# New numbers for a list scheduler: later loads, reserved buffers, gates and priorities in a recurrence + MoE kernel

## The chip, the cores and the metric

The kernel runs on one core of a Trainium2 chip. The metric is the device time of one execution in microseconds (us). The kernel before was timed three times: 1112.65, 1116.74 and 1118.03 us, median 1116.74 us. The kernel after is to be timed in the same way.

## The reference

What is computed is a recurrence over 768 steps for 4 batches of 8 heads with 40 dimensions, followed by two feed-forward networks on the 3072 x 320 result:

```
for t in range(S):
    y[:, :, t] = einsum('bhd,bhde->bhe', r_t, state)
    Sa = einsum('bhde,bhe->bhd', state, a_t)
    state = state * w_t[:, :, None, :] - einsum('bhd,bhe->bhde', Sa, b_t) + einsum('bhd,bhe->bhde', v_t, k_t)
x = y as 3072 x 320
x = relu(x @ w_in) ** 2 @ w_out                 # 320 -> 2048 -> 320   (MLP1)
out = (((x @ w1) * (x @ w2)) @ w3) @ w_out2     # 320 -> 1024 -> 320   (MLP2)
```

The weights of the two networks come in as 64-bit floats.

## The kernel before

**Units and chunks.** The recurrence is cut into 12 chunks of 64 steps, and each chunk into 4 batches. One batch of one chunk is a unit; there are 48, and unit u belongs to chunk u // 4. Two neighbouring units share a pair r = u // 2 and with it the loads of `w` and `a`; `kb` (k and b together) is loaded for each unit. Within a chunk the recurrence is a triangular system: `kn` (L384) builds it from `xl` (a times a running product of w) and `kb`, the two 32x32 halves of it are inverted, and `xu` is solved by four groups of small matmuls (L586, L600, L621, L635). `kbt` (L654) turns `kb` over, L697 makes `m`, L749 and L754 the output `y`, L723 the new state, and L668 turns state and solution over. On VectorE stand the scans of w (L310), the scaling of `kb` (L359), `xl` (L368) and the masked halves of `kn` (L394).

**The inverse.** From chunk 1 on one chain of 62 VectorE operations (31 times L526 and L531, each on the result of the one before) inverts the blocks of all four units of a chunk at once. The result `pt` goes out to DRAM (`dt`) and back in another layout (`tt`); L600 and L635 of these units read it. Chunk 0 is inverted in another way, level by level.

**MLP1 and MLP2.** When the four units of a chunk have left their `y`, it goes through DRAM (`xd`, `xraw`), is turned over and split into a high and a low part (`xh`, `xlo`), and goes through MLP1: L1016 `h` (L975 for chunk 0, with `gt` at L984), `g`, `gh` and `gl`, and the accumulation over 2048 columns at L1053 to L1055 (`acc`). MLP1 of a chunk lies beside the recurrence of later chunks. MLP2 comes at the end: the product of w3 and its output matrix (`w3p`, L1269) first, then `ab` (L1411) and `o` (L1443 to L1445). The weights are decoded by ScalarE, VectorE and GpSimd (L1620 to L1632).

**What sets the order.** Each piece of work is a step with an engine, a cost, what it reads and writes, and the buffers that it takes. `emit` (class `Plan`) puts the steps into one order with a simulated clock: on a free engine the ready step goes first whose rank is the highest. The rank is the longest chain of costs behind the step plus a weight, and the weight is `PR[kind] - later * SLOPE`, with `later` growing with the unit or the chunk. A step that needs a buffer goes only when its pools have room: `k2` has 35 buffers, `bank` has the 8 PSUM banks. `SPARE[kind]` says how many of them have to stay free after such a step; a lighter step must leave more. Before, every kind has 33 of `k2` and 6 banks there, and a flag `tight` drops all these reserves for good at the first moment at which nothing else can go. The program then issues the instructions in that order, and each engine runs its own in order. SyncE issues nearly all loads, in one order too.

**Idle matmuls.** Where the simulated clock leaves TensorE empty for longer than `IDLE`, up to the last decisive step of chunk 0's MLP1, matmuls of the identity with itself (L1119, `idle`) fill the gap. Their results are not used.

**Gates.** A load of `kb` and `a` for unit u waits in the plan for `at{u - 8}`, which is the `xu` matmul (L586) of that earlier unit; a load of `w` for pair r waits for `at{2r - 10}`.

The lines are shifted by four in the kernel after: L1016 is L1012 there, L384 is L380, L1119 is L1115.

Of the kernel before, what the change touches and what calls it, by code (L numbers as in the profile page):

```python
# [23 lines left out]
class Plan:  # L24
# [28 lines left out]
    def emit(self):  # L53
        st = self.steps
        n = len(st)
# [10 lines left out]
        used, free, dma = Counter(), dict.fromkeys("SGVAP", 0.0), 0.0  # L66
        ready, wait = [0.0] * n, {e: [] for e in "SGVAP"}
        for i, k in enumerate(st):
            if not left[i]:
                for e in k[0]:  # L70
                    wait[e].append(i)
        events, ends, order, tight = [0.0], [], [], False
        port, other = dict(V=0.0, G=0.0), dict(V="G", G="V")
        self.log = []

        def fits(i):
            take, out, opens = Counter(), [], {x for x, _ in st[i][4]}
# [12 lines left out]
        while len(order) < n:  # L90
            if not events:

                assert not tight, ("no room", used)
                tight = True
                events.append(t)
            t = heappop(events)
            while ends and ends[0][0] <= t + 1e-9:
                x = heappop(ends)[1]
# [3 lines left out]
            for e in "SGVAP":  # L102
                while free[e] <= t + 1e-9:
# [14 lines left out]
                    i, k = best, st[best]  # L118
# [40 lines left out]
def rwkv_moe(tc, wE, wF, wL, aE, kbE, rE, vE, vX, mask_d, ident_d, id32_d, eye_d, lev_d, sel_d, w_in, w_out, w1, w2, w3T, wo2_d,  # L159
             rS, kS, vS, wS, aS, bS, out):  # L160
    nc = tc.nc
    V, A, G, T, S = nc.vector, nc.scalar, nc.gpsimd, nc.tensor, nc.sync
# [69 lines left out]
    def load_w(r):  # L232
        if not once("w", r, NPAIR):
            return

        def go(tag):
            pw[r] = room(tag, [128, 8, 8, 8], f"w{r}")
            S.dma_start(out=pw[r].rearrange("p q s i -> p (q s i)"), in_=wE[r])
        step("S", 0.73, go, (f"at{2 * r - 10}",), (f"w{r}",), new=((f"w{r}", ("k2",)),))

    def load_unit(u):
        if not once("kb", u, NU):
            return
        r = u // 2

        def go(tag):
            ukb[u] = room(tag, [128, NP, 2, C], f"kb{u}")
            S.dma_start(out=ukb[u].rearrange("p q k t -> p (q k t)"), in_=kbE[u])

        def go_a(tag):  # L250
            pa[r] = room(tag, [128, 2, NP, C], f"a{r}")
            S.dma_start(out=pa[r].rearrange("p e q t -> p (e q t)"), in_=aE[r])
        step("S", 0.73, go, (f"at{u - 8}",) if u >= 8 else (), (f"kb{u}",), new=((f"kb{u}", ("k2",)),))
        if u % 2 == 0:
            step("S", 0.73, go_a, (f"at{u - 8}",) if u >= 8 else (), (f"a{r}",), new=((f"a{r}", ("k2",)),))
# [535 lines left out]
    wi = [mp.tile([128, FF], F32R, tag=f"wi{k}", bufs=1, name=f"wi{k}") for k in range(5)]  # L791
    wo = []
# [291 lines left out]

    LEAD, ITEMS = 5, 6

    PR = {'z': -1968, 'first': -376, 'l1': -4516, 'p0': -439, 'p1': 500, 'p2': -1417, 'p3': -257, 'v0': -362, 'v1': -2000, 'v2': -1452, 'v3': -2387, 'c0': -333, 'c1': -1230, 'c2': -2317, 'c3': -4652, 'o0': -1654, 'o1': 640, 'o2': -2216, 'o3': -2665, 'wi': -212, 'wo': -350, 'h0': -435, 'h1': -246, 'moe': -1909, 'st': -2657, 'pr': -2642, 'cv': -2226, 'm2': -2729}
    SPARE = {'z': {'k2': 33, 'bank': 6}, 'first': {'k2': 33, 'bank': 6}, 'l1': {'k2': 33, 'bank': 6}, 'p0': {'k2': 33, 'bank': 6}, 'p1': {'k2': 33, 'bank': 6}, 'p2': {'k2': 33, 'bank': 6}, 'p3': {'k2': 33, 'bank': 6}, 'v0': {'k2': 33, 'bank': 6}, 'v1': {'k2': 33, 'bank': 6}, 'v2': {'k2': 33, 'bank': 6}, 'v3': {'k2': 33, 'bank': 6}, 'c0': {'k2': 33, 'bank': 6}, 'c1': {'k2': 33, 'bank': 6}, 'c2': {'k2': 33, 'bank': 6}, 'c3': {'k2': 33, 'bank': 6}, 'o0': {'k2': 33, 'bank': 6}, 'o1': {'k2': 33, 'bank': 6}, 'o2': {'k2': 33, 'bank': 6}, 'o3': {'k2': 33, 'bank': 6}, 'wi': {'k2': 33, 'bank': 6}, 'wo': {'k2': 33, 'bank': 6}, 'h0': {'k2': 33, 'bank': 6}, 'h1': {'k2': 33, 'bank': 6}, 'moe': {'k2': 33, 'bank': 6}, 'st': {'k2': 33, 'bank': 6}, 'pr': {'k2': 33, 'bank': 6}, 'cv': {'k2': 33, 'bank': 6}, 'm2': {'k2': 33, 'bank': 6}}
    SLOPE = 0.832
    pl = Plan({**{k: v[1] for k, v in POOLS.items()}, "ur0": 1, "ur1": 1}, PR["st"], dict(V=V, G=G, A=A))  # L1090
    plan.append(pl)

    def go(kind, later, fn, *args):
        pl.kind = kind, later
        pl.weight = PR[kind] - later * SLOPE
        pl.spare = SPARE.get(kind, {})
        return fn(*args)
# [213 lines left out]
    n = 0  # L1311
# [410 lines left out]
```

## Time and profile before

| | before |
|---|---|
| median of 3 runs | 1116.74 us |
| profiled execution | 1114.61 us |
| its span | 1112.4 us |
| mean granted TensorE clock | 0.972 |
| PE busy | 1048.4 us (94%) |
| DVE busy | 730.2 us (66%) |
| ACT busy | 550.8 us (50%) |
| POOL busy | 118.9 us (11%) |
| chain that ended last | PE 79%, DVE 7%, DMA 5% |

The profiled execution took 2.2 us more than its span, and 2.1 us less than the median. In the profile PE is TensorE's matmuls, PEld its weight loads, DVE VectorE, ACT ScalarE, POOL GpSimd, SP or SPq SyncE and its DMA queue. A matmul's row shows when it began and how long it took; since matmuls overlap, the pitch (from one begin to the next) says what it costs. The profile keeps two records for each fp32 matmul, so a count of x34 is 17 matmuls.

### The profile page before, as it was taken

The numbers are of one execution on the slowest core, as the hardware profiler recorded it, in microseconds if no ns is written. First come the engines' busy times: TensorE is split into PE (matmuls) and PEld (weight loads), VectorE is DVE, ScalarE is ACT, GpSimd is POOL, SyncE is SP. The second block draws the span as 40 slices with busy tenths as digits, with TensorE's granted clock in tenths as the row PEclk, the third lists the DMA queues.
The fourth block names the chain that finished last, engine by engine and source line by source line (L and its number), as shares of the span: only waits on it lengthen the run. The fifth ranks groups of instructions, "written<-read, shape, count | busy, mean of one in ns | idle before, by whom it ended". The sixth has DMA issues, their size and how long they took to land.

```text
span 1112.4 us, 28437 instructions
## 1 busy us (share of the span) xinstructions
PE 1048.4 (94%) x11416; PEld 963.2 (87%) x11416; DVE 730.2 (66%) x1929; ACT 550.8 (50%) x1233; POOL 118.9 (11%) x178
## 2 busy tenths in 40 slices
PE   8999925999999899999999999999999999999996
PEld 8899825888989789898978999999998888888885
DVE  7878988877787778787888856257777332323321
ACT  3545522555555555656465665566665222222221
POOL 4442100000000000000000000023333000000000
PEclk9999966999999999999999999999999999999998
DMA  9754132534243444434525242344444310100000
GB/s 287 210 164 143 34 98 69 155 79 125 83 121 88 115 110 113 121 98 121 141 67 151 79 99 62 95 132 147 142 144 124 93 29 24 32 21 24 1 24 27
DMA packets 150403, 111.05 MB, mean 100 GB/s; under 512 B 61688, under 2 KB 130296, under 8 KB 150264
## 3 DMA queue, kind: packets, MB, share of 16 engines
q1 hardware_dynamic: 150264, 109.16, 35.4%
q8 instruction: 92, 1.51, 0.6%
q14 instruction: 47, 0.39, 0.1%
HBM read 91.88 MB, written 17.24 MB: 98 GB/s over the span
## 4 chain that ended last, share of the span: by engine, by line
PE 79%; DVE 7%; DMA 5%; ACT 2%; issue 2%; SPq 1%; POOL 1%; POOLq 0%; ACTq 0%; DVEq 0%
PE ab L1411 16%; PE h L1016 14%; PE acc L1053 4%; PE m L697 4%; PE acc L1055 4%; PE acc L1054 4%; PE kn L384 3%; PE o L1445 2%; PE o L1444 2%; PE o L1443 2%; PE w3p L1269 2%; PE idle L1119 2%; PE y L754 2%; PE y L749 2%; PE xu L586 2%
## 5 line engine op out<-in xcount | busy, mean ns | idle before, releaser
L1411 PE MATMUL ab<-x,w 128*128 128x512 f32 x768 | 183.3, 391 | 0.0
L1411 PEld LDWEIGHTS ab<-x,w 128*128 128x128 f32 x768 | 142.1, 188 | 27.4
L1016 PE MATMUL h<-xh,wi 128*128 128x256 f32 x880 | 140.9, 291 | 3.4 <-ACT xh L942 2.5
L1016 PEld LDWEIGHTS h<-xh,wi 128*128 128x128 f32 x880 | 120.0, 193 | 5.9 <-ACT xh L942 2.7
L1053 PE MATMUL acc<-wo,gh 128*128 128x320 f32 x384 | 125.0, 325 | 0.0
L1431 DVE TENSOR_TENSOR as<-ab,as 128x512 f32<-128x512 f32 x48 | 33.2, 691 | 135.4 <-PE ab L1411 135.4
L1055 PE MATMUL acc<-wo,gl 128*128 128x320 f32 x384 | 118.9, 310 | 0.5 <-DVE gl L992 0.4
L1054 PE MATMUL acc<-wo,gh 128*128 128x320 f32 x384 | 118.6, 309 | 0.0
L1032 DVE TENSOR_TENSOR gl<-g,gh 128x512 fp32r<-128x512 f32 x88 | 71.0, 808 | 36.5 <-ACT gh L1028 33.6
L526 DVE TENSOR_TENSOR ptmp<-pn,pt 128x126 f32<-128x126 f32 (+22 forms) x341 | 86.0, 252 | 11.4 <-DMA pn<-dn 2.4
L1016 PE MATMUL h<-xlo,wi 128*128 128x256 f32 x528 | 92.4, 284 | 0.0
L531 DVE TENSOR_TENSOR pt<-pt,ptmp 128x126 f32<-128x126 f32 (+22 forms) x341 | 85.9, 252 | 8.3 <-PE xu L635 0.3
L1024 ACT ACTIVATE g<-h 128x512 f32<-128x512 f32 x88 | 52.3, 597 | 62.9 <-PE h L1016 44.4
L364 POOL MEMSET xl<- 64x256 f32 x96 | 29.3, 306 | 495.3 <-PE kbt L654 59.1
L1016 PEld LDWEIGHTS h<-xlo,wi 128*128 128x128 f32 x528 | 76.4, 193 | 0.0
L1053 PEld LDWEIGHTS acc<-wo,gh 128*128 128x128 f32 x384 | 72.3, 188 | 1.7
L1055 PEld LDWEIGHTS acc<-wo,gl 128*128 128x128 f32 x384 | 72.1, 188 | 1.1 <-DVE gl L992 0.7
L1415 ACT COPY as<-ab 128x512 f32<-128x512 f32 x48 | 28.1, 586 | 90.5 <-PE ab L1411 90.4
L1054 PEld LDWEIGHTS acc<-wo,gh 128*128 128x128 f32 x384 | 72.4, 189 | 0.4 <-DVE wo L864 0.2
L1419 ACT CAST ch<-as 128x512 fp32r<-128x512 f32 x48 | 29.8, 621 | 85.9 <-DVE as L1431 85.9
L384 PE MATMUL kn<-xl,kb 128*128 128x128 f32 x384 | 52.1, 282 | 21.2 <-DVE xl L368 20.5
L384 PEld LDWEIGHTS kn<-xl,kb 128*128 128x128 f32 x384 | 47.6, 195 | 22.1 <-issue 21.5
(354 smaller groups left out, 2236.1 us busy)
## 6 DMA issues: line engine op xcount, KB each, us to landing
kb<-in_kbE_dram SPq DMA_DIRECT2D x48, 256.0 KB
t_r<-in_w3T_dram SPq DMA_DIRECT2D x16, 512.0 KB
xr<-in_vX_dram SPq DMA_DIRECT2D x48, 160.0 KB
w<-in_wE_dram SPq DMA_DIRECT2D x24, 256.0 KB
a<-in_aE_dram SPq DMA_DIRECT2D x24, 256.0 KB
rv<-in_vE_dram SPq DMA_DIRECT2D x48, 128.0 KB
pn<-dn SPq DMA_DIRECT2D x22, 256.0 KB
wor<-in_w_out_dram SPq DMA_DIRECT2D x20, 256.0 KB
```

The lines of the kernel that those rows point to most:

```text
L384: T.matmul(knp[u][:, :, p], lhsT=ukb[u][:, p].rearrange("p k t -> p (k t)"), rhs=uXL[u][:, :, p], start=True, stop=True)
L526: V.tensor_tensor(out=x, in0=pN[c][:, j:j + 1, j + 1:].to_broadcast([128, h, m]), in1=pTi[c][:, 0:h, j:j + 1].to_broadcast([128, h, m]), o ...
L531: V.tensor_tensor(out=pTi[c][:, 0:h, j + 1:], in0=pTi[c][:, 0:h, j + 1:], in1=x, op=ALU.subtract)
L697: T.matmul(m_p[0][:, hf, 2 * q:2 * q + 2], lhsT=vu[:, q, hf].rearrange("p k t -> p (k t)"), rhs=rb[:, q, :, hf], start=True, stop=True)
L1016: T.matmul(o, lhsT=wi[w][:, fs], rhs=x[:, k], start=(n == 0), stop=(n == 7))
L1024: A.activation(out=g[0], in_=hps[q], func=AF.Relu)
L1032: plan[0].now.tensor_tensor(out=g[2], in0=g[0], in1=g[1].bitcast(F32), op=ALU.subtract)
L1053: T.matmul(o, lhsT=a, rhs=wo[0][:, f], start=(f == 0), stop=False)
L1054: T.matmul(o, lhsT=a, rhs=wo[1][:, f], start=False, stop=False)
L1055: T.matmul(o, lhsT=b, rhs=wo[0][:, f], start=False, stop=(f == NF - 1))
L1411: T.matmul(ps[e], lhsT=wab[e, w, c0][:, cs], rhs=x[:, k], start=(n == 0), stop=(n == 7))
L1431: step("V", 0.62, lambda: V.tensor_tensor(out=a[0], in0=ps[1], in1=a[0], op=ALU.mult), (f"pa1{n}",), (f"as{n}",))
```

## The change

Six pieces, of which the first three are in the diff whole:

1. The flag `tight` is gone: the reserves hold to the end.
2. The load of `w` for pair r waits for the `xu` matmul of unit 2r - 9 in place of 2r - 10; the loads of `kb` and `a` for unit u wait for unit u - 7 in place of u - 8.
3. The steps of `w3p` and the load of `wl` (for a check of the inputs at the end) also need `closed`, which is written when all of the recurrence is done.
4. `PR`, the priorities, are all new.
5. `SPARE` has a reserve of its own for each kind, smaller nearly everywhere.
6. `SLOPE` is 0.728 in place of 0.832.

```
-        events, ends, order, tight = [0.0], [], [], False
+        events, ends, order = [0.0], [], []
...
-                    keep = 0 if tight else st[i][7].get(t, 0)
+                    keep = st[i][7].get(t, 0)
...
-            if not events:
-
-                assert not tight, ("no room", used)
-                tight = True
-                events.append(t)
+            assert events, ("no room", used)
...
-        step("S", 0.73, go, (f"at{2 * r - 10}",), (f"w{r}",), new=((f"w{r}", ("k2",)),))
+        step("S", 0.73, go, (f"at{2 * r - 9}",), (f"w{r}",), new=((f"w{r}", ("k2",)),))
...
-        step("S", 0.73, go, (f"at{u - 8}",) if u >= 8 else (), (f"kb{u}",), new=((f"kb{u}", ("k2",)),))
+        step("S", 0.73, go, (f"at{u - 7}",) if u >= 8 else (), (f"kb{u}",), new=((f"kb{u}", ("k2",)),))
...
-            step("S", 0.73, go_a, (f"at{u - 8}",) if u >= 8 else (), (f"a{r}",), new=((f"a{r}", ("k2",)),))
+            step("S", 0.73, go_a, (f"at{u - 7}",) if u >= 8 else (), (f"a{r}",), new=((f"a{r}", ("k2",)),))
...
-    PR = {... 'v2': -1452, ... 'h0': -435, 'h1': -246, 'moe': -1909, 'st': -2657, 'pr': -2642, 'cv': -2226, 'm2': -2729}
+    PR = {... 'v2': -1004, ... 'h0': -2452, 'h1': -1280, 'moe': -2221, 'st': -2605, 'pr': -2521, 'cv': -3171, 'm2': -4104}
-    SPARE = {'z': {'k2': 33, 'bank': 6}, ... 'moe': {'k2': 33, 'bank': 6}, 'st': {'k2': 33, 'bank': 6}, 'pr': {'k2': 33, 'bank': 6}, ...}
+    SPARE = {'z': {'k2': 33, 'bank': 6}, ... 'moe': {'bank': 1}, 'st': {'bank': 1}, 'pr': {'bank': 1}, ...}
-    SLOPE = 0.832
+    SLOPE = 0.728
...
-            step("P", 0.9, ..., tuple(f"{n}{x}" for n in (f"t{i}_{j // 4}", f"v{j}", f"v{j + 1}") for x in "hl"),
+            step("P", 0.9, ..., tuple(f"{n}{x}" for n in (f"t{i}_{j // 4}", f"v{j}", f"v{j + 1}") for x in "hl") + ("closed",),
...
-        step("S", 0.2, load_wl, (), ("wl",), (("wl", ("k2",)),))
+        step("S", 0.2, load_wl, ("closed",), ("wl",), (("wl", ("k2",)),))
```

What the tables move is shown at three places. The first is TensorE around the first solve with chunk 1's inverse (`tt1`; `xu4` to `xu7` are chunk 1's units). Before, it stands behind all of chunk 0's MLP1, and right behind the `kbt` and `kn` of chunks 1 to 3:

```order
L654 MATMUL kbt7_2129<-ident_70,kb7_1488 128x128 x4
L384 MATMUL kn12_2209<-xl12_2084,kb12_2096 128x2x64 x4
L600 MATMUL xu4_1974<-xs4_1993,tt1_2218 32x40 x8
L600 MATMUL xu5_2006<-xs5_2027,tt1_2218 32x40 x8
L600 MATMUL xu6_2066<-xs6_2112,tt1_2218 32x40 x8
L621 MATMUL xu4_1974<-us0_86,nt2_1929 32x40 x8
```

In the kernel after it stands inside chunk 0's MLP1 (`h00_8`, `gt00_4`), with runs of idle matmuls ahead of it:

```order
L971 MATMUL h00_8_1571<-wi1_96,xlo0_1500 128x512
L971 MATMUL h00_8_1571<-wi2_97,xlo0_1500 128x512
L1115 MATMUL idle_138<-ident_70 128x128 x98
L582 MATMUL xu6_1810<-xr6_1303,xl6_157 64x40 x8
L1115 MATMUL idle_138<-ident_70 128x128 x7
L596 MATMUL xu4_1435<-xs4_1456,tt1_1699 32x40 x8
L596 MATMUL xu5_1482<-xs5_1503,tt1_1699 32x40 x8
L980 MATMUL gt00_4_1864<-ident_70,g00_4_1704 128x128 x4
```

The 62 VectorE operations of chunk 1's inverse moved with it, from behind chunk 0's MLP1 into it. Idle matmuls are 159 before, of which none stands at that place, and 226 after.

The second place is TensorE at the first matmul of chunk 1's MLP1 (`h1_0`). Before:

```order
L723 MATMUL xu10_2758<-xr10_2672,kbts10_2799 40x40 x8
L668 MATMUL ut10_2997<-ident_70,us0_86 128x128 x2
L621 MATMUL xu11_2840<-us1_87,nt5_2060 32x40 x8
L668 MATMUL sz11_3015<-ident_70,sh3_85 128x128 x2
L384 MATMUL kn17_3021<-xl17_2868,kb17_2722 128x2x64 x4
L1016 MATMUL h1_0_3038<-xh1_3000,wi0_95 128x256
```

After:

```order
L1051 MATMUL acc0_1_2522<-wo_0_1195,gl01_8_2560 128x320
L980 MATMUL gt01_12_2607<-ident_70,g01_12_2587 128x128 x4
L380 MATMUL kn12_2613<-xl12_1905,kb12_1822 128x2x64 x4
L380 MATMUL kn13_2624<-xl13_2113,kb13_1895 128x2x64 x4
L1012 MATMUL h1_0_2635<-xh1_2572,wi0_95 128x256
```

Chunk 2's solve (units 8 to 11), `kn` of units 14 to 17 and the last 12 accumulations of chunk 0 stood ahead of `h1_0` before and stand behind it now; chunk 0's MLP1 and chunk 1's recurrence stand ahead of it in both.

The third is SyncE's queue around the load of `kb19`. Before:

```order
L248 DMA kb18_2877<-in_kbE_dram 128x512
L252 DMA a9_2890<-in_aE_dram 128x512
L502 DMA pn3_2903<-dn3_2443 64x1024
L277 DMA rv0_113<-in_rE_dram 40x2x128
L927 DMA xraw1_2917<-xd1_2613 128x2x256
L930 DMA xraw1_2917<-xd1_2613 64x256 x2
```

After, around `kb20`:

```order
L923 DMA xraw2_3573<-xd2_3233 128x2x256
L926 DMA xraw2_3573<-xd2_3233 64x256 x2
L234 DMA w11_3606<-in_wE_dram 128x512
L244 DMA kb20_3616<-in_kbE_dram 128x512
L248 DMA a10_3624<-in_aE_dram 128x512
L541 DMA dt3_3652<-pt3_3079 128x512
```

Beside the `xraw1` reads stood the loads for unit 18 before; beside those of `xraw2`, one chunk later, stand those for unit 20 now.

## Rows read from the trace of the kernel before

**Rows 1.** By stretch: length, busy PE, PEld, DVE, ACT, POOL; clock, DMA share, GB/s.
```profile
0.00:227.00 227.00, 186.32 (x2749) 169.55 (x2749) 182.49 (x501) 105.38 (x259) 51.83 (x82) 0.90 0.52 147
227.00:1112.40 885.40, 862.03 (x8668) 793.70 (x8668) 547.69 (x1429) 445.40 (x975) 67.10 (x96) 0.99 0.32 88
1101.97:1112.40 10.43, 0.00 (x0) 0.00 (x0) 0.00 (x0) 0.82 (x2) 0.00 (x0) 0.61 0.21 68
139.00:167.00 28.00, 7.43 (x88) 6.71 (x87) 23.29 (x84) 6.20 (x17) 1.22 (x4) 0.67 0.38 98
167.00:200.00 33.00, 21.51 (x325) 18.84 (x324) 24.97 (x89) 10.87 (x35) 0.61 (x2) 0.61 0.35 87
...
450.00:500.00 50.00, 49.20 (x608) 45.83 (x603) 43.00 (x139) 29.76 (x70) 3.06 (x10) 1.00 0.43 119
```
**Rows 2.** Timeline of PE: start, length, line, tile, [idle before <- releaser].
```profile
165.97 2.05 PE L384 MATMUL kn<-xl,kb 128*128 128x128 f32 x8 [20.53 <-DVE xl L368]
...
194.67 1.27 PE L635 MATMUL xu<-xs,tt 32*32 32x40 f32 x32 [7.67 <-DVE xs L626]
...
226.97 1.38 PE L1016 MATMUL h<-xh,wi 128*128 128x256 f32 x5 [2.47 <-ACT xh L942]
```
**Rows 3.** Timeline of DVE, chunk 1's inverse and what follows it.
```profile
145.53 0.19 DVE L526 TENSOR_TENSOR ptmp<-pn,pt 128x31 f32<-128x31 f32 x1 [1.08 <-DMA pn<-dn]
...
163.27 0.19 DVE L531 TENSOR_TENSOR pt<-pt,ptmp 128x16 f32<-128x16 f32 x1
163.49 0.86 DVE L394 TENSOR_TENSOR xl<-kn,mask 64x256 f32<-64x256 f32 x2
```
**Rows 4.** Timeline of PE at the start, the first idle matmuls.
```profile
3.71 6.39 PE L1119 MATMUL idle<-ident 128*128 128x128 f32 x34 [3.71 <-DMA ident<-in_ident_dram]
...
11.31 5.08 PE L1119 MATMUL idle<-ident 128*128 128x128 f32 x44
```
**Rows 5.** Timeline of DVE at the start, the scaling of the first kb.
```profile
8.32 0.69 DVE L359 TENSOR_TENSOR kb<-kb,suf 128x512 f32<-128x512 f32 x1 [0.23 <-DMA kb<-in_kbE_dram]
```
**Rows 6.** Timeline of PE in a dense piece at full clock.
```profile
206.69 1.16 PE L384 MATMUL kn<-xl,kb 128*128 128x128 f32 x8
207.78 0.51 PE L723 MATMUL xu<-xr,kbts 128*40 128x40 f32 x16
208.11 0.42 PE L749 MATMUL y<-rv,sz6s 128*64 128x128 f32 x4
...
209.14 1.16 PE L697 MATMUL m<-rv 128*128 128x128 f32 x8
210.13 0.38 PE L668 MATMUL ut<-ident,us 128*128 128x128 f32 x2
210.45 0.48 PE L621 MATMUL xu<-us,nt 32*32 32x40 f32 x16
210.85 0.67 PE L586 MATMUL xu<-xr,xl 128*64 128x40 f32 x16
211.45 0.66 PE L654 MATMUL kbt<-ident,kb 128*128 128x128 f32 x4
```
**Rows 7.** Twelve accumulations alone, by stretch: length, busy PE, PEld, ACT; clock.
```profile
234.33:236.09 1.76, 1.76 (x12) 1.66 (x12) 0.00 (x0) 1.00 0.00 0
```
**Rows 8.** One load of kb: SPq's issue, DVE's use, PE's use.
```profile
501.25 0.36 SPq L248 DMA_DIRECT2D kb<-in_kbE_dram  x1
503.89 0.69 DVE L359 TENSOR_TENSOR kb<-kb,suf 128x512 f32<-128x512 f32 x1 [1.05 <-DMA kb<-in_kbE_dram]
504.78 1.16 PE L384 MATMUL kn<-xl,kb 128*128 128x128 f32 x8
```
**Rows 9.** What SPq waited for: us in total, times, longest.
```profile
SPq L545 <- DVE pt L531: 60.1, 10, 22.6
```
**Rows 10.** POOL's additions of the weight decode, by form: busy, mean ns.
```profile
L1632 POOL TENSOR_TENSOR cv_t<-cv_t,before 128x512 int32<-128x512 int32 x12 | 17.9, 1496 | 30.0 <-DVE cv_t L1620 16.6 <-ACT before L1629 3.1 <-PE iw L457 2.5
L1632 POOL TENSOR_TENSOR cv_t<-cv_t,wor 128x256 int32<-128x256 int32 x20 | 17.7, 885 | 41.5 <-DVE cv_t L1620 29.9 <-ACT wor L1629 3.4 <-DVE sh L729 3.2
```

More of the change, by code (lines that the diff above doesn't have):

```diff
@@ L1085, in rwkv_moe @@
     LEAD, ITEMS = 5, 6
-    PR = {'z': -1968, 'first': -376, 'l1': -4516, 'p0': -439, 'p1': 500, 'p2': -1417, 'p3': -257, 'v0': -362, 'v1': -2000, 'v2': -1452, 'v3': -2387, 'c0': -333, 'c1': -1230, 'c2': -2317, 'c3': -4652, 'o0': -1654, 'o1': 640, 'o2': -2216, 'o3': -2665, 'wi': -212, 'wo': -350, 'h0': -435, 'h1': -246, 'moe': -1909, 'st': -2657, 'pr': -2642, 'cv': -2226, 'm2': -2729}
-    SPARE = {'z': {'k2': 33, 'bank': 6}, 'first': {'k2': 33, 'bank': 6}, 'l1': {'k2': 33, 'bank': 6}, 'p0': {'k2': 33, 'bank': 6}, 'p1': {'k2': 33, 'bank': 6}, 'p2': {'k2': 33, 'bank': 6}, 'p3': {'k2': 33, 'bank': 6}, 'v0': {'k2': 33, 'bank': 6}, 'v1': {'k2': 33, 'bank': 6}, 'v2': {'k2': 33, 'bank': 6}, 'v3': {'k2': 33, 'bank': 6}, 'c0': {'k2': 33, 'bank': 6}, 'c1': {'k2': 33, 'bank': 6}, 'c2': {'k2': 33, 'bank': 6}, 'c3': {'k2': 33, 'bank': 6}, 'o0': {'k2': 33, 'bank': 6}, 'o1': {'k2': 33, 'bank': 6}, 'o2': {'k2': 33, 'bank': 6}, 'o3': {'k2': 33, 'bank': 6}, 'wi': {'k2': 33, 'bank': 6}, 'wo': {'k2': 33, 'bank': 6}, 'h0': {'k2': 33, 'bank': 6}, 'h1': {'k2': 33, 'bank': 6}, 'moe': {'k2': 33, 'bank': 6}, 'st': {'k2': 33, 'bank': 6}, 'pr': {'k2': 33, 'bank': 6}, 'cv': {'k2': 33, 'bank': 6}, 'm2': {'k2': 33, 'bank': 6}}
-    SLOPE = 0.832
+    PR = {'z': -1957, 'first': 24, 'l1': -2220, 'p0': -1307, 'p1': -1889, 'p2': -1950, 'p3': -1977, 'v0': -1955, 'v1': -952, 'v2': -1004, 'v3': -2115, 'c0': -1540, 'c1': -4362, 'c2': -971, 'c3': -1286, 'o0': -1884, 'o1': -1892, 'o2': -1890, 'o3': -1957, 'wi': -1800, 'wo': -2148, 'h0': -2452, 'h1': -1280, 'moe': -2221, 'st': -2605, 'pr': -2521, 'cv': -3171, 'm2': -4104}
+    SPARE = {'z': {'k2': 33, 'bank': 6}, 'first': {'k2': 18, 'bank': 6}, 'l1': {'bank': 6}, 'p0': {'k2': 13, 'bank': 5}, 'p1': {'k2': 10, 'bank': 3}, 'p2': {'k2': 3, 'bank': 2}, 'p3': {'bank': 1}, 'v0': {'k2': 9}, 'v1': {'k2': 6}, 'v2': {'k2': 33, 'bank': 6}, 'v3': {'k2': 33, 'bank': 6}, 'c0': {'k2': 13, 'bank': 4}, 'c1': {'k2': 4}, 'c2': {'bank': 1}, 'c3': {'k2': 4, 'bank': 2}, 'o0': {'bank': 3}, 'o1': {'k2': 2, 'bank': 2}, 'o3': {'k2': 3, 'bank': 2}, 'wi': {'bank': 6}, 'wo': {'bank': 6}, 'h0': {'bank': 1}, 'h1': {'k2': 6, 'bank': 4}, 'moe': {'bank': 1}, 'st': {'bank': 1}, 'pr': {'bank': 1}, 'cv': {'bank': 5}, 'm2': {'k2': 12, 'bank': 2}}
+    SLOPE = 0.728
     pl = Plan({**{k: v[1] for k, v in POOLS.items()}, "ur0": 1, "ur1": 1}, PR["st"], dict(V=V, G=G, A=A))
@@ L1271, in w3_mm @@
         for j in range(0, NF2, 2):
-            step("P", 0.9, lambda *tag, j=j: go(j, *tag), tuple(f"{n}{x}" for n in (f"t{i}_{j // 4}", f"v{j}", f"v{j + 1}") for x in "hl"),
+            step("P", 0.9, lambda *tag, j=j: go(j, *tag), tuple(f"{n}{x}" for n in (f"t{i}_{j // 4}", f"v{j}", f"v{j + 1}") for x in "hl") + ("closed",),
                  (f"q{i}",), () if j else ((f"q{i}", BANK),))
```

## The prediction

> **What bounds the kernel now.** I read the busy time by engine first (the table): TensorE is busy 94% of 1112.4 us, so the whole idle time is 64 us, and a change of order can win no more than that, what a low clock costs, and the idle matmuls. Next comes the split at the first matmul of chunk 1's MLP1, at 227 us [rows 1]. After it PE is busy 862.0 of 885.4 us at clock 0.99; 10.4 of the missing 23.4 us are the tail, in which the last result is written. Ahead of it PE is busy 186.3 of 227 us, at clock 0.90. So 40.7 us of idle and all of the slow clock lie in the first fifth. PE's timeline there [rows 2] shows where: 20.5 us ahead of a `kn`, 7.7 us ahead of L635, 2.5 us ahead of the first `h`, with 3.7 us at the start [rows 4]; these make 34.4 us, and 6.3 us are crumbs. The releaser named for the 20.5 us is `xl`, but VectorE's rows say more [rows 3]: from 145.5 to 163.5 us the 62 operations of chunk 1's inverse run, 18 us of which PE can use nothing, and what PE needs next stands behind them. After this gap the granted clock of the next two stretches is 0.67 and 0.61 [rows 1], against 1.00 in the dense piece from 450 us: much of their matmul time is at 1.2 in place of 2.4 GHz. The chain of chunk 1's recurrence (inverse, solve, y, MLP1) thus bounds the first 227 us, PE's own work the rest.
>
> **The change part by part.** I cut the new program at the same instruction, the first `h1_0`.
>
> Ahead of it, the work itself. Idle matmuls: the first 17 took 6.39 us (0.376 each), later ones 5.08 us for 22 (0.231) [rows 4]; 159 of them make 6.4 + 142 x 0.231 = 39.2 us. The other PE time is 186.3 - 39.2 = 147.1 us.
>
> The slow clock. Eight records of `kn` took 2.05 us [rows 2] against 1.16 us [rows 6], 32 of L635 1.27 us against 0.80 for two groups of 16 at L621's pitch of 0.40 [rows 2, 6]: 37% to 43% of such time is excess. Of the 28.9 us busy between 139 and 200 us [rows 1] a part was at full speed still, so I take a third, 9.6 us. In the new order chunk 1's inverse stands inside chunk 0's MLP1 with 98 idle matmuls beside it (22.6 us at 0.231), so PE has work from its start to `h1_0`, and I expect this excess to go.
>
> What moves behind `h1_0`: chunk 2's solve, four `kn` and 12 accumulations. By pitches of rows 6: 4 `kn` at 1.09 = 4.4; 11 groups of L600, L621 and L635 at 0.40 = 4.4; 4 of L586 at 0.60 = 2.4; 3 of L723 at 0.33 = 1.0; 2 `m` at 0.99 = 2.0; 2 `y` at 1.03 = 2.1; 4 `kbt` at 0.66 = 2.6; 6 of L668 at 0.32 = 1.9; the accumulations 1.76 [rows 7]. Sum 22.5 us.
>
> So PE needs 147.1 - 9.6 - 22.5 = 115.0 us of work ahead of `h1_0`. Idle matmuls are now 226 at 0.231 = 52.2 us. The first PE row is now `kbt0` in place of idle matmuls; it needs the scaled `kb0`, ready at 9.0 us [rows 5], so PE starts at 9.0 in place of 3.7. The slow first steps after such a start cost as many as the 17 idle ones did, 17 x 0.145 = 2.5 us. Crumbs: half of the 6.3, 3 us. `h1_0` then comes at 9.0 + 115.0 + 52.2 + 2.5 + 3 = 181.7 us, 45 earlier.
>
> Can VectorE follow? It was busy 182.5 us ahead of `h1_0` [rows 1]. Behind it now stand 34 operations of chunk 2's inverse at 18.0 / 62 = 0.29 us (9.9), 10 of L394 and 8 of L368 at 0.43 (7.7, [rows 3]; L368 taken at the price of L394, which has the same shape), 4 scalings at 0.69 (2.8) [rows 5], three scans and some 30 small operations, which I put at 10 to 11: 31 us. The remaining 151.5 are 83% of 181.7 us, where before it kept up at 80% over 227 us and at 86% from 450 to 500 us [rows 1]. I cost it at nothing; rival B is the other end.
>
> Here a rule of the Trainium skill speaks against the change. In the rows, 32 additions of the weight decode on GpSimd take 35.6 us [rows 10], all ahead of `h1_0`, beside a VectorE that has less slack now. "SBUF — State Buffer", section "SBUF: two separate sides", says that GpSimd and VectorE share a port pair as an exclusive lock, with the later one blocked for a whole instruction when a VectorE operation reads two operands from SBUF. If every addition blocked VectorE, 151.5 + 35.6 = 187 us would not fit into 182, and the estimate would be 5 us more; no row here shows how much of it is paid.
>
> Behind `h1_0`: 885.4 us, plus 22.5 moved, 907.9. PE's own work is the same there. What can change is its 13 us of steady stalls (23.4 less the tail). The later loads add some. A load of `kb` needs 3.5 us from issue to `kn` [rows 8]. By the new order and the pitches of rows 6, PE's work between the gate's matmul and `kn` is 9.7 us at the least and 9.7 to 14.5 us for 17 of the 33 units from 15 on; before it was mostly 19 to 53. So an undelayed load is in time by 6 us, and only one that waits on SyncE behind something else is late. That happens: SyncE waited up to 22.6 us for an inverse before it could issue its store [rows 9], with whatever stood behind it. The bounds are nothing, and 33 us for a delay that makes each gate-to-`kn` way 14.5 us (rival C). I take 4 us, near the low end, since the measured way is 3.5. `closed` on `w3p` and `load_wl` I cost at nothing: `w3p` began behind the recurrence's end anyway, and now that end comes sooner by one chunk's step of MLP1; PE has MLP1 of the last chunks to do meanwhile. If that cover were gone, `w3p`'s start would show a wait. The missing `tight` has no instruction; it acts only through the order.
>
> Sum: 181.7 + 907.9 + 4 = 1093.6 us of span, against 1112.4. The profiled execution was 2.2 us over its span, so 1095.8 against 1114.6; the median was 2.1 over that, so about **1098 us**.
>
> **The rivals.**
>
> A. The steady stalls shrink too. The reserves keep buffers for the heavier steps, so of the 13 us of steady stalls 8 might go in place of 4 coming, and the idle matmuls run at 0.22: 1098 - 4 - 8 - 2 = about 1084, and 1078 if the crumbs go too. For it: a new order for the whole program. Against it: 50 us stretches with 49.2 busy leave little [rows 1].
>
> B. VectorE becomes the bound ahead of `h1_0`. Idle matmuls fill what the plan's clock leaves empty; where VectorE is later than the plan, PE waits on top of them. At the 80% of before, 151.5 us take 189 us, 7.7 later than my 181.7, and the same lag, with a stall in the denser piece up to chunk 1's end (22.5 us more PE work beside 31 us more of VectorE), costs up to 8 more: 1106 to 1114. For it: the 20.5 us gap was VectorE's. Against it: 86% in steady state.
>
> C. The later loads turn into a wait; this ends slower. SyncE issues in order, and a `kb` behind a store that waits for an inverse comes late; then `kn`, the inverse and the whole chain behind wait. Priced over the 33 units: if the way from gate to `kn` takes 12 us the stalls sum to 5 us, at 14 to 25, at 14.5 to 32, at 15 to 41. Slower than before from about 13.7 us on, where the 19 us of gain are used up; taken at 14.5, 1094 + 32 = 1126 us. For it: SyncE's long waits [rows 9]. Against it: the measured way of 3.5 us [rows 8].
>
> D. The early gap doesn't go: the inverse stands earlier but its inputs (`pn`, through DRAM) come later than planned, so that the 98 idle matmuls run ahead of it and PE waits as before, again at the low clock. Then 18 us and 9.6 us come back on top of the 67 added idle matmuls: 1098 + 28 = 1126 us, slower as well. Against it: the inverse began 1.1 us after its input in the rows [rows 3].
>
> **How the numbers follow.** My forecast 0.60 (own range 1088 to 1107), A 0.13, B 0.14, C 0.08, D 0.05. What a measurement of this kernel tells from no change is about 0.5%, 5.6 us, so faster means under 1111.2 and slower above 1122.3. Faster: 0.57 of the forecast's 0.60, all of A, 0.07 of B: 0.77. Within 0.5%: 0.02, 0.06 of B and 0.02 of C and D: 0.10. Slower: the rest, 0.13. The range takes in most of A and B and the milder end of C: 1078 to 1120.
>
> **What would show it.** Right: `h1_0` near 182 us; no PE gap of 20 us; the inverse of chunk 1 beside idle matmuls; clock near 1.00 in the stretch from 20 to 200 us; PE idle after `h1_0` about 27 us, tail included. B shows as PE waits on VectorE ahead of `h1_0`, with VectorE over 85% busy. C shows as PE or VectorE waits for `kb` or `xl` after 200 us. D shows as a PE gap behind the long run of idle matmuls and a clock near 0.6. A wrong forecast would be seen first in the idle time after `h1_0`, of which I could only bound the change.

## The result and the profile after

The kernel after takes 1085.3 us in the median (1083.42 to 1092.35, 4 runs) against 1117.38 us for the kernel before (1112.65 to 1119.11, 4 runs): a ratio of 0.9731, 95% interval 0.9678 to 0.9784. Run again later, the same kernel took 1081.9 us (6 runs), ratio 0.9708 (0.9666 to 0.9749). The profiled execution has a span of 1084.4 us, 28.0 us less than before. The head of its page answers to the table of before:

```profile
span 1084.4 us, 28692 instructions
PE 1050.4 (97%) x11550; PEld 967.1 (89%) x11550; DVE 714.7 (66%) x1929; ACT 551.6 (51%) x1233; POOL 118.7 (11%) x178
```

TensorE is busy for 2 us more than before and the span is 28 us shorter, so idle time went. The stretches, cut at the first `h` of chunk 1's MLP1 as in [rows 1] (columns as there):

```profile
0.00:187.83 187.83, 170.63 (x2459) 158.01 (x2459) 155.92 (x421) 90.19 (x216) 49.96 (x76) 1.00 0.55 154
187.83:1084.40 896.57, 879.73 (x9095) 809.07 (x9093) 558.76 (x1509) 461.40 (x1018) 68.70 (x102) 1.00 0.33 92
...
28.00:56.00 28.00, 23.11 (x594) 21.96 (x594) 20.96 (x36) 11.39 (x21) 12.14 (x11) 1.00 0.72 193
...
111.00:139.00 28.00, 27.91 (x347) 26.68 (x347) 23.55 (x85) 8.39 (x24) 5.16 (x7) 1.00 0.32 85
139.00:167.00 28.00, 27.30 (x353) 24.93 (x350) 24.20 (x62) 19.59 (x53) 7.58 (x10) 1.00 0.56 153
```

The cut lies at 187.8 us in place of 227. By the prediction's sum 22.5 us of PE work moved behind it, so the net gain ahead of it is 39.2 - 22.5 = 16.7 us. Behind it 896.6 us stand against 885.4 + 22.5 = 907.9: another 11.3 us. The two make the 28.0. The granted clock is 1.00 in all of these stretches. The two timelines, of PE and then of DVE, that answer to [rows 2] and [rows 3]:

```profile
6.96 1.11 PE L650 MATMUL kbt<-ident,kb 128*128 128x128 f32 x4 [6.96 <-DVE kb L355]
...
109.38 22.05 PE L1115 MATMUL idle<-ident 128*128 128x128 f32 x196
...
187.83 0.84 PE L1012 MATMUL h<-xh,wi 128*128 128x256 f32 x5
```
```profile
109.48 0.19 DVE L522 TENSOR_TENSOR ptmp<-pn,pt 128x31 f32<-128x31 f32 x1 [0.81 <-DMA pn<-dn]
...
127.19 0.19 DVE L527 TENSOR_TENSOR pt<-pt,ptmp 128x16 f32<-128x16 f32 x1
```

Chunk 1's inverse runs from 109.5 to 127.4 us, 36 us earlier, with 98 idle matmuls beside it (0.225 us each). The gaps of 20.5, 7.7 and 2.5 us are gone. What PE waits for behind the cut, in the kernel before and then in the one after (us in total, times, longest), the four greatest of each:

```profile
PE m L697 <- ACT rv L671: 4.9, 4, 2.6
PE xu L600 <- DMA tt<-dt: 2.6, 2, 1.9
PE h L1016 <- ACT xh L942: 2.5, 1, 2.5
PE w3p L1269 <- ACT t_0h L1245: 0.8, 1, 0.8
```
```profile
PE xu L631 <- DVE xs L622: 1.2, 4, 0.4
PE kn L380 <- ACT kbts L654: 1.0, 1, 1.0
PE kn L380 <- DVE xl L364: 0.9, 2, 0.5
PE xu L596 <- DMA tt<-dt: 0.8, 1, 0.8
```

### The profile page after: what moved, and what is told of

Read it like the earlier page. It is cut to its first block, busy times and chain, and to the rows that moved or that the text cites. A ratio compares the mean times of both kernels' runs of the same rounds, so it can differ in the third digit from the quotient of the medians.

```text
span 1084.4 us, 28692 instructions
## 1 busy us (share of the span) xinstructions
PE 1050.4 (97%) x11550; PEld 967.1 (89%) x11550; DVE 714.7 (66%) x1929; ACT 551.6 (51%) x1233; POOL 118.7 (11%) x178
## 5 line engine op out<-in xcount | busy, mean ns | idle before, releaser
L1012 PEld LDWEIGHTS h<-xh,wi 128*128 128x128 f32 x880 | 117.8, 190 | 2.6 <-ACT g L1020 0.2
L1028 DVE TENSOR_TENSOR gl<-g,gh 128x512 fp32r<-128x512 f32 x88 | 62.4, 709 | 36.0 <-ACT gh L1024 33.5
L1024 ACT CAST gh<-g 128x512 fp32r<-128x512 f32 x88 | 54.5, 619 | 12.8 <-PE y L745 4.1
L390 DVE TENSOR_TENSOR xl<-kn,mask 64x256 f32<-64x256 f32 x96 | 40.5, 422 | 30.4 <-ACT nt L398 18.2
```

Source lines behind the costliest of these rows:

```text
L390: V.tensor_tensor(out=uXL[u][o:o + 64, hf], in0=knp[u][o:o + 64, hf], in1=mask[o:o + 64].unsqueeze(1).to_broadcast([64, NP, C]), op=ALU.mult)
L1012: T.matmul(o, lhsT=wi[w][:, fs], rhs=x[:, k], start=(n == 0), stop=(n == 7))
L1024: A.copy(out=g[1], in_=g[0])
L1028: plan[0].now.tensor_tensor(out=g[2], in0=g[0], in1=g[1].bitcast(F32), op=ALU.subtract)
```

## The experiments

The theories. T: ahead of the cut the chain through chunk 1's inverse and solve sets the time, and the new numbers put it earlier; behind the cut the gain comes from what the new numbers do there. Rivals: the clock is the early gain; the later loads are the gain, or the danger; the better start alone gives the rest. Each ratio below is against executions of the kernel before taken together with that run (medians 1111.3 to 1117.4 us); what a run differs by from the kernel after is reckoned from 1085.3 or 1081.9 us.

**Idle matmuls out of the kernel after (e1_no_late_idle).** Each run of idle matmuls planned behind 100 us is left out, 116 in all:

```
-                    self.idle(int((t - at) / self.IDLE))
+                    self.idle(int((t - at) / self.IDLE) if t < 100 else 0)
```

> The kernel after, without the 116 idle matmuls that it issues from the start of chunk 1's inverse on (among them the run of 98). Theory: these matmuls keep TensorE at its higher clock through a stretch in which VectorE works alone; without them TensorE is empty for about 22 us, the granted clock falls to 0.5, and part of the 55 us of dense work up to the first h1_0 runs at half pace: 1094 to 1105 us, h1_0 at 195 to 208 us, clock under 0.8 in the stretch behind the gap. Rival: the gain is only that the inverse lies earlier, idle matmuls do nothing: 1085 us, h1_0 at 188.

Measured: 1089.7 us (4 runs), ratio 0.9779 (0.9709 to 0.9848), which overlaps the kernel after's interval. The trace is clearer: PE's wait for the inverse, and four stretches behind its start.

```profile
132.85 1.28 PE L596 MATMUL xu<-xs,tt 32*32 32x40 f32 x32 [23.15 <-DMA tt<-dt]
```
```profile
110.00:131.00 21.00, 0.00 (x0) 0.00 (x0) 19.13 (x74) 1.84 (x5) 1.69 (x2) 0.59 0.11 32
...
135.00:140.00 5.00, 4.78 (x87) 3.93 (x88) 2.06 (x8) 2.97 (x10) 2.04 (x4) 0.50 0.58 172
140.00:150.00 10.00, 10.00 (x122) 8.87 (x122) 5.46 (x14) 5.25 (x16) 1.71 (x2) 0.50 0.32 91
150.00:160.00 10.00, 10.00 (x154) 9.09 (x153) 8.29 (x23) 8.15 (x22) 2.77 (x5) 0.93 0.51 134
```

The clock does fall, to half (1.2 GHz) until about 150 us. But `h1_0` comes at 191.6 us, only 4 to 7 us later than in four executions with this order (184.6 to 187.8). How much of that is the clock can be read over one stretch that every such execution has, from the first solve with chunk 1's inverse (the L596 of the row above, which begins at 133.71 us in the kernel after) to `h1_0`; in the kernel after and then in this one:

```profile
133.71:187.83 54.12, 53.22 (x646) 47.81 (x645) 46.42 (x134) 33.52 (x85) 10.92 (x16) 1.00 0.43 119
```
```profile
132.85:191.61 58.76, 57.89 (x622) 52.00 (x623) 46.13 (x134) 33.98 (x86) 10.95 (x16) 0.84 0.40 111
```

The other three executions of the first order take 53.7 to 54.1 us for it. So the low clock costs 4.6 us here, although 11 idle matmuls fewer lie in the stretch. The expectation, 9 to 20 us, was two to four times too high; by this stretch its rival, no loss at all, is out too.

**The gaps of the kernel before bridged (e2_bridge, e5_bridge_right).** Two kernels; the first put 86 idle matmuls ahead of `kn12`, 33 ahead of L635 of unit 8 and 10 ahead of `h1_0`:

```
             if tag:
                 knp[u] = room(tag[0], [128, 2, NP, C], f"kn{u}")
+                if u == 12:
+                    for _ in range(86):
+                        T.matmul(knp[u][:, :, 0], lhsT=ident, rhs=ident, start=True, stop=True)
```

> The kernel before in its own order, with 129 idle matmuls more, put into its three gaps ahead of h1_0 (86 ahead of kn12, 33 ahead of L635 of unit 8, 10 ahead of h1_0). Theory: the slow clock there costs time, but VectorE's two inverses bound most of this stretch, so 4 to 10 us come back: 1108 to 1113 us, granted clock near 1.00 from 139 to 240 us. Rival: VectorE alone bounds this stretch and TensorE's clock is off the path: 1115 to 1119 us. Second rival: the clock is the whole early gain (17 us or more): 1100 us or less.

Measured: 1118.7 us (10 runs), ratio 1.0050 (1.0014 to 1.0086). Unit 8's L635 lies behind the second gap, so those 33 were pure cost (7.5 us at 206.6). Behind the cut, where nothing was changed, this execution took 879.3 us in place of 885.4, at full clock. The second kernel moved them to unit 6 and dropped the last 10:

> The kernel before in its own order, with 84 idle matmuls ahead of kn12 and 32 ahead of L635 of unit 6, where its two gaps of 20.5 and 7.7 us lie; the second run of e2_bridge had stood ahead of unit 8, behind that gap. If the slow clock in that stretch costs time of its own: 4 to 8 us less than before, 0.993 to 0.996 of it, and clock near 1.00 from 139 to 227 us. If VectorE bounds the stretch so that the clock is off the path, as e2_bridge hinted: 0.998 to 1.003. More than 9 us less would make the clock the main part of the early gain.

Measured: 1118.4 us (11 runs), ratio 1.0047 (1.0023 to 1.0071). Its second bridge failed as well; its first one fills its gap. PE's timeline:

```profile
150.87 18.92 PE L385 MATMUL kn<-ident 128*128 128x128 f32 x168
171.37 1.13 PE L387 MATMUL kn<-xl,kb 128*128 128x128 f32 x8 [1.58 <-issue]
...
199.72 9.68 PE L637 MATMUL xu<-ident 128*128 128x128 f32 x64 [7.66 <-DVE xs L629]
```

The 32 idle matmuls of unit 6 write to the tile from which VectorE still reads; they waited for VectorE with the rest and came behind the gap. What can be read is the stretch from `kn12` to the end of that gap, in the kernel before ([rows 2]) and then in this one:

```profile
165.97:194.67 28.70, 17.49 (x252) 15.32 (x253) 23.22 (x87) 8.47 (x26) 0.61 (x2) 0.62 0.27 67
```
```profile
171.37:199.72 28.35, 16.29 (x252) 14.24 (x252) 23.28 (x87) 8.47 (x26) 0.61 (x2) 0.66 0.27 68
```

`kn12` itself ran at full clock (1.13 us in place of 2.05), but the clock did not stay up: behind further waits of 2.1 and 1.2 us it was 0.66 in the mean, against 0.62 before. So the 0.35 us between the two stretches do not say what a full clock would be worth there. VectorE is busy for 23 of the 28 us in both, and PE's 7.7 us at the end are a wait for VectorE, so that VectorE's next inverse sets this stretch is likely; it is argued and not shown. Besides, the profiled execution took 1130.8 us, the slowest of the eleven. What the clock's share was in the kernel before stays open; the total times say only that these two kernels lose about what their misplaced idle matmuls cost.

**Still later loads (e3_loads_u6).** Gates at u - 6 and 2r - 8, with the two changes of the tables that leave room for it (`wi` -1578, one bank kept back by `v1`):

```
-        step("S", 0.73, go, (f"at{u - 7}",) if u >= 8 else (), ...
+        step("S", 0.73, go, (f"at{u - 6}",) if u >= 8 else (), ...
```

> The kernel after with its loads gated still later (kb and a on unit u - 6, w on 2r - 8), which needs two small changes of the tables to leave room for all buffers (wi -1578, one PSUM bank kept back by v1). The planned way from gate to kn falls from 8.8 to 25 us to 4.4 to 13.7 us, half of the units under 6.6 us; idle matmuls are 263 in place of 226 and h1_0 is planned 9 us later. Theory (a load needs 3.5 us from issue to kn): later loads cost little, so 1085 + 9 = 1094 us, 1090 to 1100, with under 15 us of waits for kb or xl behind h1_0. Rival (the way from gate to kn takes 12 to 14 us on the chip, so that the gates of the change are at the edge): 33 units late by 5 us or more each, 1150 us or more.

Measured: 1085.0 us (4 runs), ratio 0.9761 (0.9687 to 0.9836), the same as the kernel after. Its stretches:

```profile
0.00:191.50 191.50, 179.78 (x2573) 166.94 (x2574) 162.74 (x444) 93.55 (x222) 49.76 (x78) 1.00 0.56 154
191.50:1080.70 889.20, 874.57 (x9053) 805.80 (x9052) 549.55 (x1486) 456.81 (x1011) 67.71 (x100) 1.00 0.33 92
```

The idle time of VectorE ahead of a scaling that waits for its load of `kb`, in the kernel before, the kernel after and this one (us, times):

```profile
  DMA kb<-in_kbE_dram: 6.7, 7
```
```profile
  DMA kb<-in_kbE_dram: 3.3, 3
```
```profile
  DMA kb<-in_kbE_dram: 1.1, 3
```

The rival in which the gates are at their edge is wrong by over 60 us: even with half of the planned ways under 6.6 us next to nothing waits. The expected 1094 us were 9 too many: `h1_0` came 4 us later and not 9, and the stretch behind it is 7 us shorter, 5 us of which are PE work that stands ahead of `h1_0` here.

**One priority put back: c3 (e4_c3_undone).**

```
-    PR = {... 'c3': -1286, ...}
+    PR = {... 'c3': -4652, ...}
```

> The kernel after with one priority put back, c3 (the solve of units 6 and 7) from -1286 to -4652, nothing else. Chunk 1's last two units then come later, and h1_0 about 19 us later in the plan, with 237 idle matmuls in place of 226. Theory: the time of h1_0 is the gain, so nearly all of the 19 us is paid: 1099 to 1106 us. Rival: TensorE only does other work first and gets the time back behind h1_0: 1085 to 1091 us.

Measured: 1104.2 us (10 runs), ratio 0.9917 (0.9886 to 0.9947). PE's timeline at the cut:

```profile
208.08 1.23 PE L1012 MATMUL h<-xh,wi 128*128 128x256 f32 x4 [7.45 <-ACT xh L938]
```

`h1_0` is 20 us later and the whole 19 us later than 1085.3: the time of `h1_0` is paid in full, as T said. The stretch behind it is 894.2 us, 2.4 us shorter than in the kernel after, with 3.6 us less PE work in it, so nothing comes back there.

**The old numbers from 240 us on (e6_old_numbers_later).** The plan runs with the new tables to 240 us and then with those of before:

```
+            if tight is None and t >= 240.0:
+                rank = [x - k[6] + k[9] for x, k in zip(rank, st)]
+                heavy, keeps, tight = [k[9] for k in st], [k[10] for k in st], False
+                self.patient = PR2["st"]
```

> The kernel after up to 240 us of the plan (some 60 us behind h1_0), and from there on the priorities, SLOPE and reserves (with tight) of the kernel before; gates as in the kernel after. Theory: the 11 us that were won behind h1_0 come from what the new numbers do there (fewer stalls and no low clock behind them), so with the old numbers they are lost: 1095 to 1103 us, h1_0 still near 188, PE idle behind h1_0 over 25 us. Rival: they follow from the better start alone: 1083 to 1089 us.

Measured: 1095.1 us (4 runs), ratio 0.9836 (0.9787 to 0.9886). The stretches, and two short ones in which the clock fell:

```profile
0.00:184.57 184.57, 171.22 (x2458) 158.75 (x2459) 155.44 (x421) 90.23 (x216) 50.06 (x76) 1.00 0.55 156
184.57:1092.50 907.93, 887.66 (x9095) 813.26 (x9093) 559.57 (x1509) 461.31 (x1018) 70.24 (x102) 0.99 0.33 91
```
```profile
250.00:300.00 50.00, 48.26 (x583) 45.12 (x583) 33.89 (x107) 26.32 (x59) 1.83 (x6) 0.93 0.31 80
800.00:820.00 20.00, 17.80 (x106) 16.73 (x106) 14.64 (x23) 13.18 (x24) 6.73 (x4) 0.91 0.40 114
```

Behind the cut it takes 907.9 us, what the kernel before took for the same work. PE is idle there for 20.3 us, less than the 25 expected, and busy for 8 us more than in the kernel after with the same instructions. So the better start alone doesn't give the 11 us; the new numbers are needed behind the cut. They are not lost where the kernel before lost them, though: the low clocks of that kernel stand at other times (shown below, where the prediction's failed term is told), so this run says that the new numbers are needed, and not which waits they removed.

**One priority put back: cv (e7_decode_early).**

```
-    PR = {... 'cv': -3171, ...}
+    PR = {... 'cv': -2226, ...}
```

> The kernel after with one priority put back, cv (decode of MLP2's weights) from -3171 to -2226, nothing else; the order is the same up to long after h1_0. Theory: VectorE is over 83% busy until the recurrence ends, so decoding beside it delays the recurrence and TensorE waits: 1094 to 1102 us, h1_0 at 188 us, and the added idle time between 450 and 750 us. Rival: VectorE has room, the decode is hidden: 1083 to 1088 us.

Measured: 1095.8 us (4 runs), ratio 0.9834 (0.9785 to 0.9882), `h1_0` at 185.8 us. From 700 to 800 us, in this kernel and then in the kernel after:

```profile
700.00:800.00 100.00, 92.27 (x646) 90.53 (x645) 63.43 (x98) 63.56 (x111) 35.60 (x25) 0.97 0.46 137
```
```profile
700.00:800.00 100.00, 100.00 (x742) 100.00 (x741) 64.21 (x103) 69.47 (x122) 35.30 (x24) 1.00 0.49 144
```

and its waits of PE in this stretch:

```profile
PE acc L1051 <- DVE gl L1028: 5.8, 4, 3.6
PE w3p L1265 <- ACT t_0h L1241: 1.6, 1, 1.6
```

The size was right, the place was not: nothing is lost up to 700 us, where the recurrence is done. The loss is in the last chunks' MLP1, whose `gl` stands behind the decoding in VectorE's order. VectorE was not full there (63.4 of 100 us); it waited itself, 13.5 us of it for ScalarE's part of the decoding (9.9 in the kernel after).

**The load gates alone (e8_gates_alone)**, in the kernel before, everything else as it was:

> The kernel before with the later load gates alone (kb and a on unit u - 7, w on 2r - 9); all numbers, reserves and tight as before. Theory: the gates bring nothing by themselves, the numbers do, and numbers made for the other gates fit badly: 1115 to 1140 us, h1_0 at 220 us or later. Rival: the later loads free buffers and that is the gain: 1085 to 1105 us.

Measured: 1142.7 us (4 runs), ratio 1.0244 (1.0187 to 1.0300), `h1_0` at 233.9. The old gap is there, and greater, on PE's timeline:

```profile
176.14 1.68 PE L600 MATMUL xu<-xs,tt 32*32 32x40 f32 x44 [22.97 <-DMA tt<-dt]
```

The gates by themselves gain nothing; with the old numbers they cost 2.4%, a little more than the range expected.

**Chunk 1's inverse made longer (e9_double_inverse, e12_double_bridged)** in the kernel after:

```
+            for _ in range(2 if c == 1 else 1):
                 V.tensor_tensor(out=x, in0=pN[c][:, j:j + 1, j + 1:]..., op=ALU.mult)
```

> The kernel after, with each of the 31 products of chunk 1's inverse (L522, 7.9 us in all) issued twice on VectorE; the order on all engines else the same, and the second product writes the same numbers again. Theory: ahead of h1_0 VectorE's chain sets the time, and the inverse is in it, so TensorE waits behind its idle matmuls and h1_0 comes 6 to 8 us later; as nothing behind h1_0 gives it back, the whole takes 1090 to 1094 us. Rival: TensorE's own work and the idle matmuls set the time ahead of h1_0 and the inverse has slack: 1083 to 1087 us.

Measured: 1097.7 us (4 runs), ratio 0.9851 (0.9797 to 0.9906), 12 to 16 us more than the kernel after for 7.9 us of VectorE. PE's timeline and stretches, the last from the first solve to `h1_0`:

```profile
140.01 1.27 PE L597 MATMUL xu<-xs,tt 32*32 32x40 f32 x32 [8.12 <-DMA tt<-dt]
```
```profile
131.00:150.00 19.00, 10.88 (x166) 9.29 (x166) 12.94 (x44) 9.63 (x27) 5.16 (x7) 0.63 0.50 139
150.00:160.00 10.00, 10.00 (x133) 9.06 (x133) 5.76 (x16) 5.41 (x16) 1.78 (x3) 0.68 0.25 72
...
140.00:155.00 15.00, 14.99 (x204) 12.94 (x205) 8.11 (x23) 7.53 (x24) 3.48 (x5) 0.50 0.51 153
...
140.01:200.40 60.39, 59.72 (x644) 53.86 (x645) 46.70 (x134) 33.78 (x86) 10.79 (x16) 0.86 0.38 108
```

PE waits 8.1 us, the clock falls, and `h1_0` comes at 200.4 us, 13 to 16 us later. To tell the wait from the clock, the run of 98 idle matmuls was made 134 long:

```
-                    self.idle(int((t - at) / self.IDLE))
+                    n = int((t - at) / self.IDLE)
+                    self.idle(n + 36 if n > 90 else n)
```

> e9_double_inverse with 36 idle matmuls more (134 in place of 98) beside chunk 1's inverse, so that TensorE is not empty while it waits the 8.1 us that the doubled products cost. e9 lost 14 us for 7.9 us of VectorE; the question is the other 6. If they are the low clock behind the gap (0.63 and 0.68 granted from 131 to 160 us in e9): granted clock 1.00 throughout, h1_0 at 195 to 197 in place of 200.4 us, 1089 to 1094 us. If they are not: h1_0 at 200 and 1096 to 1099 us, as in e9.

Measured: 1095.2 us (1089.4 to 1099.2, 4 runs), ratio 0.9844 (0.9784 to 0.9904): by the times not told apart from the one before. The profiled execution took 1089.4 us, with `h1_0` at 191.7 and the clock at full:

```profile
131.00:150.00 19.00, 18.70 (x326) 16.79 (x324) 15.12 (x44) 13.51 (x39) 6.78 (x9) 1.00 0.63 177
...
138.01:191.73 53.72, 53.05 (x645) 47.80 (x645) 45.91 (x133) 33.43 (x85) 10.91 (x16) 1.00 0.43 121
```

The traces tell the two apart. From the first operation of the inverse to the first solve both kernels take 8 to 9 us more than the kernel after (32.7 and 33.3 us against 23.8 to 24.8 in four executions): the doubled products and the wait for them. From the first solve to `h1_0` it is 60.4 us with the low clock and 53.7 without, for the same PE instructions: the low clock cost 6.7 us. That the idle matmuls hold the clock is shown, and what that is worth in this stretch, in one execution of each; `h1_0` came earlier than the 195 to 197 us expected because the inverse began 2.6 us earlier in this execution than in that of e9_double_inverse. Over the whole time four runs of each don't show the difference.

**A version meant to be faster (e11_searched)**, run beside the kernel after:

> The kernel after as it is, for comparison on the same chip: 1083 to 1088 us.

> The gates of e3_loads_u6 (u - 6 and 2r - 8) with priorities, reserves and SLOPE searched anew for them, 232 idle matmuls. In e3_loads_u6 the stretch behind h1_0 took 889 us against 897 in the kernel after, but h1_0 came at 191.5; the new numbers put it 9 us earlier in the plan. If both hold on the chip: 1074 to 1080 us. If the chip does not follow the plan at that size: 1081 to 1088 us, no faster than the kernel after.

Measured: 1081.9 us (6 runs) for the kernel after, 1082.8 us (6 runs), ratio 0.9725 (0.9679 to 0.9770), for the searched numbers. `h1_0` came at 185.2 us, as hoped, but the stretch behind it took 897.0 us, not 889, with PE idle for 19.8 us of it against 14.6 in e3_loads_u6. None of these kernels beats the kernel after.

## Why the prediction was right, and which term was wrong

The direction, the place of the early gain and its cause (chunk 1's inverse earlier, with PE busy beside it) were right; 1098 us was 13 us too high, the time lies within the range and just outside the forecast's own range, at the size of rival A (1084). In the span the forecast's 1093.6 us became 1093.6 + 6.1 - 4 - 11.3 = 1084.4: late ahead of the cut, no cost of the loads, and a gain behind it that the sum didn't have. That the first error took back a part of the others is luck. The other 3.4 us are what the prediction added to the span, 4.3 us, where the median of this kernel is 0.9 us above its profiled span. By steps:

**Ahead of `h1_0`** the sum gave 181.7 us, the trace 187.8 (184.6 to 187.8 over four executions). The work held: 115.0 + 52.2 + 2.5 = 169.7 us against 170.6 measured. The start was better (7.0 us in place of 9.0), the crumbs worse, 10.2 us where 3 were forecast: PE was idle 3.9 us from 7 to 28 us, and busy only 23.1 of 28 us from 28 to 56 us, in chunk 0's own inversion (26.5 in the trace of e12_double_bridged, so this differs between executions). In all it was idle for 17.2 us where 12 were forecast.

**The slow clock, 9.6 us.** As PE time it was about right: the clock is at full and the work came out as summed. Whether it was a gain of its own in the kernel before stays open, since neither bridge kept the clock up there. That a low clock can cost its time ahead of the cut is shown in the kernel after: 4.6 us without the idle matmuls (e1_no_late_idle), 6.7 us between e9_double_inverse and e12_double_bridged.

**VectorE costed at nothing.** It was busy 155.9 of 187.8 us, 83% as forecast, and rival B's lag didn't come. But the chain has no slack: 7.9 us more in the inverse put the first solve 8 to 9 us later, and with the low clock behind that wait it cost 12 to 16. The exclusive port lock that the Trainium skill states ("SBUF — State Buffer", section "SBUF: two separate sides") is the rule by which the prediction's estimate was 5 us more. This case's trace agrees with it in kind: in the kernel after, some VectorE operations that began inside one of GpSimd's additions ended only behind it, as this one, which otherwise takes 0.46 us (a decode step with one operand, where the prediction spoke of two):

```profile
28.05 1.41 POOL L1628 TENSOR_TENSOR cv_t<-cv_t,before 128x512 int32<-128x512 int32 x1 [0.50 <-ACT iw L466]
```
```profile
28.27 1.48 DVE L1616 TENSOR_SCALAR cv_t<-before 128x512 int32<-128x512 int32 x1
```

Ahead of `h1_0`, the VectorE operations that were clearly lengthened so lasted in all 3.4 us longer than the median of their kind, and 3.6 us in the kernel before (estimates from the two engines' timelines in both kernels). So VectorE paid about the same in both, and this does not explain the 6 us that `h1_0` came late.

**The term that failed** is the last: "So an undelayed load is in time by 6 us ... I take 4 us" for the stretch behind `h1_0`. It was 11.3 us the other way. The loads cost nothing, as e3_loads_u6 shows with gates still later. And the steady stalls, which the prediction left in place, shrank: PE idle behind the cut is 16.8 us against 23.4, which without the tail of each is 6.2 against 13.0, and PE busy 879.7 against 862.0 + 22.5 = 884.5. The second part are low clocks that came with stalls of the kernel before. The prediction had put all of the slow clock ahead of the cut; these rows, which it didn't read, have some 4.5 us of it behind (busy time times what is missing of the clock, an estimate), where the kernel after has none:

```profile
227.00:240.00 13.00, 13.00 (x90) 13.00 (x91) 11.81 (x36) 9.54 (x20) 0.00 (x0) 0.87 0.33 89
350.00:400.00 50.00, 45.48 (x643) 41.34 (x644) 36.34 (x110) 26.38 (x67) 2.45 (x8) 0.97 0.45 120
...
550.00:600.00 50.00, 47.28 (x642) 42.97 (x640) 39.43 (x128) 27.34 (x70) 1.83 (x6) 0.97 0.44 119
```

With the old numbers from 240 us on, the 11 us are gone (907.9 us); with only `cv` put back, 10.7 us are gone (907.2). So the new numbers are needed behind the cut. The second run shows that with them the decoding has to stay late; it doesn't show what the kernel before lost, which has the same `cv` and leaves PE idle for only 1.1 us from 700 to 800 us. Which of the other numbers matter was not tried. The 11.3 us are one pair of executions: behind the cut the new order took 895.2 to 896.6 us in five traces (the kernel after twice, e1_no_late_idle, e9_double_inverse and e12_double_bridged), the order of before 879.3, 885.4 and 888.7 in three (e2_bridge, the kernel before, e5_bridge_right), which with the 22.5 us makes 5 to 16 us.

**The gates** alone make the kernel before slower (1.0244). With the new tables they make room in the plan: a later load holds its buffer for less time, and with the gates of before the new tables leave the plan without a free `k2` buffer at 137 us of its clock. So "tables with the old gates" could not be tried as a part. `closed` on `w3p` costs nothing: without it the plan is the same.

**Rivals.** C and D, the slower ones, are out: C by e3_loads_u6, D by the trace (no gap behind the 98 idle matmuls). B's lag has nearly the size of the 6.1 us, but not its sign, PE waits on VectorE with VectorE over 85% busy. A was the one whose size came, and its mechanism in part: the steady stalls shrank by 6.8 us, where it had put 8; the low clock behind the cut, which no rival named, was the rest.

## What to carry to other kernels

Where a list scheduler sets the order, cut the trace at one instruction that both orders have, sum the work ahead of it and behind it apart, and don't leave the steady stretch at "as before": its stalls of 1 to 3 us, with the clock that falls behind them, were worth two thirds of the early gain here. A wait can cost more than its own length, since the clock falls behind it: take one stretch of the same instructions at full and at low clock to see how much (53.7 to 54.1 us against 58.8 and 60.4 here), and look whether a filler really kept the clock up before reading anything from it. A knob that costs when tried alone (the gates) can still be what makes the good order fit.

## What the hardware showed that was not expected

An 8.1 us wait of TensorE left the granted clock at its lower level (0.50) for 15 us, from 140 to 155 us, though PE was busy throughout (e9_double_inverse); after a 23 us wait it was 0.50 until about 150 us, 17 us behind its end (e1_no_late_idle). Idle matmuls that were put into the PSUM tile `xu6`, of which VectorE had still to read other columns, waited 7.66 us for VectorE (e5_bridge_right), where those put into the fresh tile of `kn12` didn't; whether the chip or only the program's own semaphores asked for that wait is not told apart. Executions of one kernel scatter by up to 1.4% here, and the slower ones have the lower mean clock (kernel before, 19 runs: 1106.0 us at 0.977, 1121.1 us at 0.966), so a few us can't be read from the median of four runs; stretches of the same instructions that several traces share (53.7 to 54.1 us, 895.2 to 896.6 us) serve better.
